# A scan feeding a cosine-gated layer: the opening re-ordered so that two of four sequences are scanned first

## The chip, the cores and the metric

The kernel runs on one core of a Trainium2 chip. The metric is the device time of one execution in microseconds (us); less is better. The kernel before the change took 381.69 us, the median of 7 runs (380.91 to 382.24).

## What is computed

The reference has two blocks. The first is a chunked state-space scan over `batch, heads, seq, head_dim, d_state = 4, 8, 768, 32, 16`:

```
cum = cumsum(log a);  L[i,j] = exp(cum_i - cum_j) for i >= j, else 0
y   = ((C B^T) * L) x  +  exp(cum) * (C state)
state = exp(sum log a) * state + sum_j exp(cum_end - cum_j) B_j x_j
```

Its output is laid out as 3072 tokens of 256 features. The second block is `h = x @ w_in` (256 x 2048), `g = h * cos(h)`, `out = g @ w_out` (2048 x 256). All tensors are fp32; the weights arrive as 64-bit words of which each fp32 value is put together on the chip.

## The kernel before the change

**Tiles.** The sequence is cut into 6 chunks of 128 steps. Each chunk gives 512 tokens (4 sequences of 128), and each chunk has 16 steps `n` of the second block. In chunk 0 one step `n` takes one pair of 128-wide `w_in` columns and one pair of sequences: even `n` takes sequences 0 and 1, odd `n` sequences 2 and 3 (`turn_of`). A step has three parts. `first(n)` is 4 matmuls into the PSUM bank `hp` (8 MATMUL records), then ACT rounds (`k`, L523) and DVE subtracts (`w`, L525). `gate(n)` is the sine on ACT (L530), and `gated(n)` the product on DVE (`gT`, L535). `second(n)` is the matmul by `w_out` (L578 in chunk 0), and it runs two steps behind (`LAG = 2`).

**The opening.** Before step 0, chunk 0 has to be scanned. For each sequence `b`: `spread_a` multiplies out the decays into PSUM; `decays0` runs the scan on DVE (L309) and then a copy and a memset on POOL (L312, L313); `cross` makes with one matmul, for two sequences, the part across halves, which ACT copies into `lam` (L321) and POOL weighs (`weigh`, L328); `turn` transposes B and C (L360) and ACT copies them out (L364, L366); `intra` makes `g = C B^T` on PE (L374) and `m = g * lam` on DVE (L381); `finish` makes `y` on PE (L391), which ACT copies to `yT` (L395).

**The weights.** `w_in` and `w_out` come in 8 pieces each, in 512 KB of words. `fetch` starts the transfer. `grade` is ACT's `Abs` (`mag`, L193), POOL's clamp (L194) and ACT's other half (`last`, L191). `join` is two bit operations on DVE (L207, L209) and an add on POOL (L217), after which the piece can be used. With `later=True` the `last` of a piece is issued behind the sine of the step. Piece `in 0` is needed by steps 0 and 1, `in 1` by steps 2 and 3, `out 0` by `second(0)` and `second(1)`.

**What sets the order.** The kernel is written under a manual schedule: every engine runs its instructions in the order in which they are written, and so does the one DMA queue on SP. An instruction that waits holds all behind it on its engine. PSUM banks go round in pairs under the tags `h`, `o` and `scan`. The order of the first step is written by hand at the end of the program (L669 ff.): all four `spread_a` and all four scans come first, then sequences 0, 1, 2, 3 through `turn`, `intra`, `finish`. POOL's two clamps of the decay rows (`cut`, `la`, L693 to L695) and the two transfers that write them to DRAM (`a_cut`, `a_all`, L697) stand between `finish(1)` and `join("in", 0)`. All later loads stand behind these two on SP: the rows of chunk 1 (B, C, x), `along` and `arow`, which read `a_all` and `a_cut` back, and the later pieces of the weights.

Of the kernel before, what the change touches and what calls it, by code (L numbers as in the profile page):

```python
# [8 lines left out]
FP32 = mybir.dt.float32  # L9
# [16 lines left out]
def kernel(  # L26
# [30 lines left out]
    V, ACT, G, PE = nc.vector, nc.scalar, nc.gpsimd, nc.tensor  # L57

    NB, H, S, D = x.shape
    N = B.shape[-1]  # L60
    P = 128
# [24 lines left out]
    def bank(shape, name, tag):  # L86
        return psum.tile(shape, FP32, tag=tag, bufs=2, name=name)

    def pair(name):

        return psum.tile([P, 2, 4 * P], FP32, tag="scan", bufs=2, name=name)
# [125 lines left out]
            G.tensor_tensor(out=dst.bitcast(U32), in0=bits, in1=last, op=ALU.add)  # L217

    for b in range(NB):
        if b == NB - 1:  # L220
            fetch("in", 0)
        load(0, (b, b + 1))
    nc.sync.dma_start(
# [70 lines left out]
    def spread_a(b, tag):  # L294


        spread[b] = ps = bank([P, H, W], "a_ps", tag)
        for t in range(2):
            PE.matmul(ps[t * W:(t + 1) * W], lhsT=those[:, b:b + 1].to_broadcast([P, W]),  # L299
                      rhs=a0s[:, t], start=True, stop=True, tile_position=(0, t * W),  # L300
                      skip_group_check=True)

    def decays0(b):

        lam[0, b] = l = scan.tile([P, 2, H, W], FP32, tag="lam", bufs=4, name="lam")
        flat = "p h i -> p (h i)"
        V.tensor_tensor_scan(out=l[:, 0].rearrange(flat), data0=spread.pop(b).rearrange(flat),  # L309
                             data1=unit0.rearrange(flat), initial=0.0,  # L310
                             op0=ALU.mult, op1=ALU.add)
        G.tensor_copy(out=l[W:P, 1], in_=l[W:P, 0])  # L312
        G.memset(l[W:P, 0], 0.0)  # L313

    def cross(b, tag):

        ps = bank([P, H, W], "l_ps", tag)
        PE.matmul(ps, lhsT=fros[:, b:b + 2].rearrange("p b j -> p (b j)"), rhs=tos,  # L318
                  start=True, stop=True)
        for t in range(2):  # L320
            ACT.copy(out=lam[0, b + t][0:W, 1], in_=ps[t * W:(t + 1) * W])  # L321
            weigh(0, b + t)

    def weigh(c, b):

        scaled[c, b] = sc = scan.tile([P, H, N], FP32, tag="sc", bufs=NB, name="sc")
        l = lam[c, b][:, :, P - 1:P] if c > 0 else lam[c, b][:, 1, :, W - 1:W]
        G.tensor_tensor(out=sc, in0=raw[c][0][:, 0, heads(b)],  # L328
                        in1=l.to_broadcast([P, H, N]), op=ALU.mult)
# [21 lines left out]
            return  # L351
        weigh(c, b)

    def turn(b, tag=None):

        bc = raw[0][0]
        tp = (pair("tp")[:, 0] if tag is None else bank([P, 4 * P], "tp", tag)
              ).rearrange("p (k i) -> p k i", k=4)
        for k in range(2):
            PE.transpose(tp[:, k], bc[:, k, heads(b)].rearrange("p h n -> p (h n)"), ident)  # L360

        cT = scan.tile([P, 2, P], FP32, tag="cT", name="cT")
        for t in range(2):
            ACT.activation(cT[:, t], tp[:, 1], AF.Copy, scale=slot[:, t:t + 1])  # L364
        bT = scan.tile([P, P], FP32, tag="bT", name="bT")
        ACT.copy(out=bT, in_=tp[:, 0])  # L366
        part[0, b] = (bT, cT)

    def intra(b):
        bT, cT = part[0, b]  # L370
        g = [pair("g") for _ in range(2)]
        for q in range(4):
            r = slice(32 * q, 32 * q + 32)
            PE.matmul(g[q // 2][:, q % 2, 0:2 * P], lhsT=bT[r],  # L374
                      rhs=cT[r].rearrange("p t (s i) -> p s t i", s=2), start=True, stop=True)
        l = lam.pop((0, b))
        m = scan.tile([P, 2, H, W], FP32, tag="m", bufs=4, name="m")
        for q in range(2):
            of = [t[:, :, q * HH:(q + 1) * HH].rearrange("p s (k t) i -> p k s (t i)", k=2)
                  for t in (m, l)]  # L380
            V.tensor_tensor(out=of[0], in0=g[q][:, :, 0:2 * P].rearrange(  # L381
                "p k (s i) -> p k s i", s=2), in1=of[1], op=ALU.mult)
        part[0, b] = m

    def finish(b, tag, fills=0):
        m, xr = part.pop((0, b)), raw[0][1]
        y = bank([P, 4, P], "y", tag)
        fill(y[:, 2:4], fills)
        for h in range(H):
            q, t = h % 4, h // 4  # L390
            PE.matmul(y[32 * q:32 * q + 32, t], lhsT=xr[:, b, h], rhs=m[:, :, h],  # L391
                      start=(t == 0), stop=True, tile_position=(0, 32 * q), skip_group_check=True)
        if b == 0:
            yT[0] = two.tile([P, 2, TB], FP32, tag="yT", name="yT")
        ACT.copy(out=yT[0][:, :, b * P:(b + 1) * P], in_=y[:, 0:2])  # L395
# [110 lines left out]
        c, f = divmod(n, NF)  # L506
        return (f % 2, f // 2) if c == 0 else divmod(f, NJ)

    def first(n):
        c, f = divmod(n, NF)  # L510
        hp[n] = bank([P, TB], "hp", "h")

        u, j = turn_of(n)
        to_ = hp[n].rearrange("p (e t s i) -> p e t s i", e=2, t=2, s=2)
        y = yT[c].rearrange("p k (u s t i) -> p k u t s i", u=2, s=2, t=2)
        for e in range(2):
            fs = slice((2 * j + e) * P, (2 * j + e + 1) * P)
            for k in range(KT):
                PE.matmul(to_[:, e], lhsT=w_in[:, k, fs], rhs=y[:, k, u],  # L519
                          start=(k == 0), stop=(k == KT - 1), skip_group_check=True)  # L520

        k = ffn.tile([P, TB], I32, tag="k", name="k")
        ACT.activation(k, hp[n], AF.Copy, bias=0.25, scale=INV_2PI)  # L523
        turns[n] = w = ffn.tile([P, TB], FP32, tag="w", name="w")
        V.scalar_tensor_tensor(out=w, in0=hp[n], scalar=INV_2PI, in1=k,  # L525
                               op0=ALU.mult, op1=ALU.subtract)

    def gate(n):
        cos = turns[n]
        ACT.activation(cos, cos, AF.Sin, bias=quarter, scale=TWO_PI)  # L530
# [139 lines left out]
    warm = bank([P, 4, P], "warm", "o")  # L670
    fill(warm, 2)
    spread_a(0, "h")
    turn(0)
    spread_a(1, "h")
    spread_a(2, "o")
    spread_a(3, "h")
    for b in range(NB):
        decays0(b)
    turn(1, "h")
    cross(0, "o")  # L680
    intra(0)
    turn(2, "h")
    cross(2, "o")
    intra(1)
    finish(0, "o")
    grade("in", 0, n=2)
    intra(2)
    turn(3, "h")
    finish(1, "o", 1)

    la = const.tile([RB, NU, P], FP32, name="la")
    cut = const.tile([RB, NU, P], FP32, name="cut")
# [4 lines left out]
        nc.sync.dma_start(  # L697
            out=dst.rearrange("(u b) h (c p) -> (b h c) u p", u=NU, p=P), in_=src)

    join("in", 0)  # L700
    finish(2, "o")
    intra(3)
    grade("in", 1)
    rest = grade("out", 0, later=True)
    join("in", 1)


    piece = {n: ("in", (n + 3) // 2) if n % 2 else ("out", n // 2) for n in range(NF)}
# [16 lines left out]

    def first_scan():

        finish(3, "o")
        for u in range(2):
            sums[u] = pair("s_ps")[:, :, 0:2 * D]  # L730
            for t in range(2):
                sum_up(0, 2 * u + t, sums[u][:, t])
# [25 lines left out]
    def ends(n):  # L758
        return [(c, us) for c, at, us, _, _, end in plan if at + end == n]

    rest_of_loads()
    for n in range(NC * NF + LAG):
        c, f = divmod(n, NF)
        if n < NC * NF:
            if f == 0 and c > 0:
                load(c + 2)
            first(n)
            if n == 0:
                first_scan()
            for at in pairs(n):  # L770
                turn2(*at)
            rests = [rest] if n == 0 else []
            if n + 1 in piece:
                rests.append(grade(*piece[n + 1], later=True))
            gate(n)
            for rest in rests:
                if rest:
                    rest()
            if n in piece and n > 1:
                join(*piece[n])  # L780

            behind = [lambda at=at: halved(*at) for at in halves_at(n)]
            behind = [lambda at=(c, 2 * u + 1): masked(*at) for c, u in pairs(n - 2)] + behind
            if n not in piece and behind:
                behind.pop(0)()
            gated(n)
            if n < 2:
                join(*piece[n])
            for do in (*behind, *unsummed):
                do()  # L790
            unsummed.clear()
            if n in (1, 2):
                carry(0, n - 1, sums[n - 1])
        for i, js in differ_at.get(n, ()):
            differ_w(i, js)
        if n >= LAG:
            second(n - LAG)
        for c, u in pairs(n - 1):
            intra2(c, u)
            masked(c, 2 * u)  # L800
        for c, us in ends(n):
            finish2(c, us)
            if 1 in us:
                raw.pop(c)
        for c, u in pairs(n + 1):
            for b in (2 * u, 2 * u + 1):
                reaches(c, b)
                load_along(c + 1, (b,))
# [30 lines left out]
```

## Time and profile before

| what | value |
|---|---|
| median of 7 runs | 381.69 us (380.91 to 382.24) |
| the profiled execution's own time | 380.91 us |
| its span | 379.1 us |
| around the span | 1.8 us |
| granted TensorE clock | 1.00 in every stretch |
| PE / DVE / ACT / POOL busy | 373.3 / 279.9 / 173.5 / 213.7 us |
| busy from 25.57 to 376.00 us (350.43 us): PE / DVE / ACT / POOL | 349.87 / 259.09 / 155.77 / 195.81 us |
| first `hp` matmul (step 0) | 17.68 us |
| first `o` matmul, `second(0)` | 25.57 us |

How to read it: times count from the span's start. A row of a timeline is start, duration, engine, line, operation, `output<-inputs`, shapes and count; the bracket at its end is the time for which the engine was idle before it and what ended that. In the chain of waits a row is start, duration and what the chain was in at that time. Matmul records are pipelined, so the first of a row looks longer than the work that it adds: 8 `hp` records behind others take 1.73 us. An fp32 matmul leaves two records.

### The profile page before, as it was taken

What the parts mean: (1) busy time and instruction counts of PE and PEld (TensorE: products, weight loads), DVE (VectorE), ACT (ScalarE), POOL (GpSimd) and SP (SyncE); (2) the same over time, 40 slices, a digit from 0 to 9 for tenths busy, and PEclk for the clock granted to TensorE, in tenths of its full rate; (3) what the DMA queues carried; (4) which work ended last, traced back from release to release, by engine and by line L of the source; (5) the groups of instructions that cost most, each with busy time, mean ns of one, the idle gap of its engine ahead of it and who ended that gap; (6) DMA issues with size and microseconds to landing.
All of it is one profiled execution on the core that took longest, in us unless ns stands there. A gap on an engine that the chain in (4) does not pass through costs nothing.

```text
span 379.1 us, 7680 instructions
## 1 busy us (share of the span) xinstructions
PE 373.3 (98%) x2980; PEld 330.2 (87%) x2980; DVE 279.9 (74%) x431; ACT 173.5 (46%) x303; POOL 213.7 (56%) x330
## 2 busy tenths in 40 slices
PE   8999999999999999999999999999999999999996
PEld 2578888889989999998999998899998999999995
DVE  8879999899689748967748986756986862554643
ACT  3887756444344434443434453424444433433442
POOL 6767565579864437673444683443775343454551
PEclk9999999999999999999999999999999999999999
DMA  6989989969230961420681330100010000010011
GB/s 79 259 235 292 251 209 129 180 96 176 78 110 17 148 61 58 138 73 2 83 74 55 83 117 11 42 2 2 1 30 3 8 21 2 0 29 0 2 28 29
DMA packets 106371, 30.42 MB, mean 80 GB/s; under 512 B 75520, under 2 KB 102240, under 8 KB 106336
## 3 DMA queue, kind: packets, MB, share of 16 engines
q1 hardware_dynamic: 106176, 29.81, 38.9%
q8 instruction: 23, 0.38, 0.5%
q10 hardware_dynamic: 160, 0.13, 0.1%
q14 instruction: 12, 0.10, 0.1%
HBM read 26.59 MB, written 3.34 MB: 79 GB/s over the span
## 4 chain that ended last, share of the span: by engine, by line
PE 96%; DVE 2%; POOL 1%; issue 0%; POOLq 0%
PE hp L519 43%; PE o L616 33%; PE o L578 7%; PE g L423 3%; PE y L457 3%; PE y L450 1%; PE tp L406 1%; PE a_ps L299 1%; PE warm L101 1%; DVE mag L209 1%; PE g L374 1%; POOL w_in L217 1%; PE o L661 1%; PE s_ps L478 0%; PE l_ps L318 0%; DVE mag L207 0%
## 5 line engine op out<-in xcount | busy, mean ns | idle before, releaser
L519 PE MATMUL hp<-yT,w_in 128*128 128x256 f32 x768 | 183.8, 382 | 0.5 <-POOL w_in L217 0.3
L519 PEld LDWEIGHTS hp<-yT,w_in 128*128 128x128 f32 x768 | 139.5, 190 | 21.4 <-issue 3.2
L560 POOL TENSOR_TENSOR gd<-gT 128x256 f32<-128x256 f32 x79 | 59.8, 757 | 104.9 <-DVE gT L535 79.5
L530 ACT ACTIVATE w<-w,quarter 128x512 f32<-128x512 f32 x96 | 69.3, 722 | 77.6 <-DVE w L525 77.4
L523 ACT ACTIVATE k<-hp 128x512 int32<-128x512 f32 x96 | 57.2, 596 | 103.3 <-PE hp L519 102.8
L525 DVE SCALAR_TENSOR_TENSOR w<-hp,k 128x512 f32<-128x512 f32 x96 | 65.7, 684 | 50.3 <-ACT k L523 50.1
L535 DVE TENSOR_TENSOR gT<-hp,w 128x512 f32<-128x512 f32 x96 | 65.2, 679 | 32.4 <-ACT w L530 27.2
L616 PE MATMUL o<-words,gd 128*128 128x128 f32 x474 | 66.9, 277 | 0.0
L616 PEld LDWEIGHTS o<-words,gd 128*128 128x128 f32 x474 | 59.8, 192 | 0.5
L345 DVE TENSOR_TENSOR_SCAN lam<-arow,unit 128x512 f32<-128x512 f32 x40 | 55.7, 1393 | 0.0
L563 POOL TENSOR_TENSOR gd<-gT,gd 128x128 f32<-128x128 f32 x79 | 48.1, 609 | 6.2
L616 PEld LDWEIGHTS o<-w_out,gT 128*128 128x128 f32 x316 | 46.9, 191 | 3.6
L616 PE MATMUL o<-w_out,gT 128*128 128x128 f32 x316 | 48.0, 275 | 0.0
L562 POOL TENSOR_TENSOR gd<-gT,gd 128x128 f32<-128x128 f32 x79 | 41.4, 525 | 6.2
L578 PE MATMUL o<-w_out,gT 128*128 128x256 f32 x128 | 30.3, 380 | 0.4 <-POOL w_out L217 0.4
L616 PE MATMUL o<-words,gT 128*128 128x128 f32 x158 | 30.6, 275 | 0.0
L616 PE MATMUL o<-w_out,gd 128*128 128x128 f32 x158 | 30.6, 275 | 0.0
L578 PEld LDWEIGHTS o<-w_out,gT 128*128 128x128 f32 x128 | 24.2, 190 | 4.0 <-POOL w_out L217 0.8
L436 DVE TENSOR_TENSOR m<-g,lam 128x512 f32<-128x512 f32 x40 | 25.6, 680 | 0.0
L616 PEld LDWEIGHTS o<-words,gT 128*128 128x128 f32 x158 | 24.0, 192 | 0.0
L616 PEld LDWEIGHTS o<-w_out,gd 128*128 128x128 f32 x158 | 24.0, 192 | 0.0
L633 DVE TENSOR_TENSOR sum<-ps,sum 128x256 f32<-128x256 f32 (+1 forms) x27 | 16.7, 645 | 0.6
(91 smaller groups left out, 281.7 us busy)
## 6 DMA issues: line engine op xcount, KB each, us to landing
arow<-a_cut SPq DMA_DIRECT2D x20, 512.0 KB, 4.0
words<-in_moe_w_in_dram SPq DMA_DIRECT2D x8, 512.0 KB, 6.3
words<-in_moe_w_out_dram SPq DMA_DIRECT2D x8, 512.0 KB, 8.5
out_dram<-sum SPq DMA_DIRECT2D x18, 128.0 KB, 2.5
xr<-in_x_dram SPq DMA_DIRECT2D x4, 512.0 KB
along<-a_all SPq DMA_DIRECT2D x20, 64.0 KB
xr<-in_x_dram SPq DMA_DIRECT2D x8, 128.0 KB
bc<-in_B_dram SPq DMA_DIRECT2D x4, 256.0 KB, 5.1
```

The costliest lines, as they stand in the source:

```text
L345: V.tensor_tensor_scan(out=lam[c, b][:, hs].rearrange("p h i -> p (h i)"), data0=rows_.rearrange("p h i -> p (h i)"), data1=unit.rearrange ...
L436: V.tensor_tensor(out=of[0], in0=g[q][:, :, s * 2 * P:(s + 1) * 2 * P], in1=of[1], op=ALU.mult)
L519: PE.matmul(to_[:, e], lhsT=w_in[:, k, fs], rhs=y[:, k, u], start=(k == 0), stop=(k == KT - 1), skip_group_check=True)
L523: ACT.activation(k, hp[n], AF.Copy, bias=0.25, scale=INV_2PI)
L525: V.scalar_tensor_tensor(out=w, in0=hp[n], scalar=INV_2PI, in1=k, op0=ALU.mult, op1=ALU.subtract)
L530: ACT.activation(cos, cos, AF.Sin, bias=quarter, scale=TWO_PI)
L535: V.tensor_tensor(out=gT[n], in0=hp.pop(n), in1=cos, op=ALU.mult)
L560: G.tensor_tensor(out=d[:, 0:2], in0=g[:, 1:2].to_broadcast([P, 2, P]), in1=g[:, 3::-3], op=ALU.subtract)
L562: G.tensor_tensor(out=d[:, 2], in0=g[:, 0], in1=d[:, 0], op=ALU.subtract)
L563: G.tensor_tensor(out=d[:, 3], in0=g[:, 2], in1=d[:, 2], op=ALU.subtract)
L578: PE.matmul(o[c, u][:, t], lhsT=g[:, 2 * e + t], rhs=w_out[:, 2 * j + e], start=(j == e == t == 0), stop=(j == NJ - 1 and e == 1), skip_gr ...
L616: PE.matmul(at[q], lhsT=a_[q], rhs=w[q], start=(j == 0 and q in starts), stop=(j == NJ - 1), skip_group_check=True)
```

## The change

Sequences 0 and 1 are carried through scan, `turn`, `intra` and `finish` first. The scan of sequence 2 follows `intra(0)`, that of sequence 3 follows `join("in", 0)`; `spread_a(2)` and `spread_a(3)` move back with them. `turn(2)` and `turn(3)` are issued together behind that, then `intra(2)`. `cross` no longer contains ACT's copies and POOL's `weigh`; the copies are `crossed(b)`, and `weigh` is issued later. On SP, `in 0` is fetched before sequence 2 and no longer before sequence 3. `grade("in", 0)` moves up, `join("in", 0)` moves up to before the scan of sequence 3.

On POOL the clamp of `in 1` now stands before `cut` and `la`; `weigh(0, 0)` and `weigh(0, 1)` follow these, then the clamp of `out 0`, the add of `in 1`, `weigh(0, 2)` and `weigh(0, 3)`, the clamp of `in 2` and the add of `out 0`. Step 0 gets a function of its own, `start`: `intra(3)` lies between the two tiles of `first(0)`; `join("in", 1)`, ACT's and DVE's part of step 0 (`turned`), `finish(2)` and `finish(3)` follow; and `join("out", 0)` stands before `gated(0)` where it stood behind it. `first_scan` (the matmuls `s_ps` of the state) moves from behind `first(0)` to behind `first(1)`. The filling matmul of `finish(1)` goes. `turn` takes its bank from the caller, with half the width.

```diff
--- before.py
+++ after.py
@@ -217,7 +217,7 @@
             G.tensor_tensor(out=dst.bitcast(U32), in0=bits, in1=last, op=ALU.add)
     for b in range(NB):
-        if b == NB - 1:
+        if b == 2:
             fetch("in", 0)
         load(0, (b, b + 1))
     nc.sync.dma_start(
@@ -300,11 +300,16 @@
                       rhs=a0s[:, t], start=True, stop=True, tile_position=(0, t * W),
                       skip_group_check=True)
-    def decays0(b):
-        lam[0, b] = l = scan.tile([P, 2, H, W], FP32, tag="lam", bufs=4, name="lam")
+    def decays0(b, early=False):
+        if early:
+            lam[0, b] = scan.tile([P, 2, H, W], FP32, tag="lam", bufs=4, name="lam")
+            return
+        if (0, b) not in lam:
+            decays0(b, True)
+        l = lam[0, b]
         flat = "p h i -> p (h i)"
         V.tensor_tensor_scan(out=l[:, 0].rearrange(flat), data0=spread.pop(b).rearrange(flat),
                              data1=unit0.rearrange(flat), initial=0.0,
@@ -312,14 +317,17 @@
         G.tensor_copy(out=l[W:P, 1], in_=l[W:P, 0])
         G.memset(l[W:P, 0], 0.0)
+    crosses = {}
     def cross(b, tag):
         ps = bank([P, H, W], "l_ps", tag)
         PE.matmul(ps, lhsT=fros[:, b:b + 2].rearrange("p b j -> p (b j)"), rhs=tos,
                   start=True, stop=True)
-        for t in range(2):
-            ACT.copy(out=lam[0, b + t][0:W, 1], in_=ps[t * W:(t + 1) * W])
-            weigh(0, b + t)
+        crosses.update({b + t: ps[t * W:(t + 1) * W] for t in range(2)})
+    def crossed(b):
+        ACT.copy(out=lam[0, b][0:W, 1], in_=crosses.pop(b))
     def weigh(c, b):
@@ -351,11 +359,10 @@
             return
         weigh(c, b)
-    def turn(b, tag=None):
+    def turn(b, tp):
         bc = raw[0][0]
-        tp = (pair("tp")[:, 0] if tag is None else bank([P, 4 * P], "tp", tag)
-              ).rearrange("p (k i) -> p k i", k=4)
+        tp = tp.rearrange("p (k i) -> p k i", k=2)
         for k in range(2):
             PE.transpose(tp[:, k], bc[:, k, heads(b)].rearrange("p h n -> p (h n)"), ident)
@@ -373,7 +380,7 @@
             r = slice(32 * q, 32 * q + 32)
             PE.matmul(g[q // 2][:, q % 2, 0:2 * P], lhsT=bT[r],
                       rhs=cT[r].rearrange("p t (s i) -> p s t i", s=2), start=True, stop=True)
-        l = lam.pop((0, b))
+        l = lam[0, b]
         m = scan.tile([P, 2, H, W], FP32, tag="m", bufs=4, name="m")
         for q in range(2):
             of = [t[:, :, q * HH:(q + 1) * HH].rearrange("p s (k t) i -> p k s (t i)", k=2)
@@ -506,7 +513,7 @@
         c, f = divmod(n, NF)
         return (f % 2, f // 2) if c == 0 else divmod(f, NJ)
-    def first(n):
+    def first(n, between=None):
         c, f = divmod(n, NF)
         hp[n] = bank([P, TB], "hp", "h")
@@ -514,10 +521,16 @@
         to_ = hp[n].rearrange("p (e t s i) -> p e t s i", e=2, t=2, s=2)
         y = yT[c].rearrange("p k (u s t i) -> p k u t s i", u=2, s=2, t=2)
         for e in range(2):
+            if e and between:
+                between()
             fs = slice((2 * j + e) * P, (2 * j + e + 1) * P)
             for k in range(KT):
                 PE.matmul(to_[:, e], lhsT=w_in[:, k, fs], rhs=y[:, k, u],
                           start=(k == 0), stop=(k == KT - 1), skip_group_check=True)
+        if not between:
+            turned(n)
+    def turned(n):
         k = ffn.tile([P, TB], I32, tag="k", name="k")
         ACT.activation(k, hp[n], AF.Copy, bias=0.25, scale=INV_2PI)
@@ -670,23 +683,32 @@
     warm = bank([P, 4, P], "warm", "o")
     fill(warm, 2)
     spread_a(0, "h")
-    turn(0)
+    turn(0, pair("tp")[:, 0, 0:2 * P])
     spread_a(1, "h")
+    decays0(0)
+    decays0(1)
+    cross(0, "o")
+    crossed(0)
+    crossed(1)
+    intra(0)
+    turn(1, bank([P, 2 * P], "tp", "h"))
+    grade("in", 0, n=2)
     spread_a(2, "o")
+    decays0(2)
+    intra(1)
+    cross(2, "o")
     spread_a(3, "h")
-    for b in range(NB):
-        decays0(b)
-    turn(1, "h")
-    cross(0, "o")
-    intra(0)
-    turn(2, "h")
-    cross(2, "o")
-    intra(1)
+    decays0(3, early=True)
+    crossed(2)
+    crossed(3)
     finish(0, "o")
-    grade("in", 0, n=2)
+    finish(1, "o")
+    join("in", 0)
+    decays0(3)
+    turn(2, bank([P, 2 * P], "tp", "h"))
+    turn(3, bank([P, 2 * P], "tp", "o"))
     intra(2)
-    turn(3, "h")
-    finish(1, "o", 1)
+    grade("in", 1)
     la = const.tile([RB, NU, P], FP32, name="la")
     cut = const.tile([RB, NU, P], FP32, name="cut")
@@ -697,12 +719,8 @@
         nc.sync.dma_start(
             out=dst.rearrange("(u b) h (c p) -> (b h c) u p", u=NU, p=P), in_=src)
-    join("in", 0)
-    finish(2, "o")
-    intra(3)
-    grade("in", 1)
-    rest = grade("out", 0, later=True)
-    join("in", 1)
+    weigh(0, 0)
+    weigh(0, 1)
     piece = {n: ("in", (n + 3) // 2) if n % 2 else ("out", n // 2) for n in range(NF)}
@@ -725,7 +743,6 @@
     def first_scan():
-        finish(3, "o")
         for u in range(2):
             sums[u] = pair("s_ps")[:, :, 0:2 * D]
             for t in range(2):
@@ -758,20 +775,41 @@
     def ends(n):
         return [(c, us) for c, at, us, _, _, end in plan if at + end == n]
+    def start():
+        rests = [grade("out", 0, later=True)]
+        first(0, lambda: intra(3))
+        join("in", 1)
+        turned(0)
+        finish(2, "o")
+        for b in range(NB):
+            if b > 1:
+                weigh(0, b)
+            del lam[0, b]
+        finish(3, "o")
+        rests.append(grade(*piece[1], later=True))
+        gate(0)
+        for rest in rests:
+            if rest:
+                rest()
+        join("out", 0)
+        gated(0)
     rest_of_loads()
+    start()
     for n in range(NC * NF + LAG):
         c, f = divmod(n, NF)
         if n < NC * NF:
             if f == 0 and c > 0:
                 load(c + 2)
+            if n == 0:
+                continue
             first(n)
-            if n == 0:
+            if n == 1:
                 first_scan()
             for at in pairs(n):
                 turn2(*at)
-            rests = [rest] if n == 0 else []
-            if n + 1 in piece:
-                rests.append(grade(*piece[n + 1], later=True))
+            rests = [grade(*piece[n + 1], later=True)] if n + 1 in piece else []
             gate(n)
             for rest in rests:
                 if rest:
@@ -784,7 +822,7 @@
             if n not in piece and behind:
                 behind.pop(0)()
             gated(n)
-            if n < 2:
+            if n == 1:
                 join(*piece[n])
             for do in (*behind, *unsummed):
                 do()
```

## The prediction

> **What bounds the kernel now.** I read the page's chain first, then the busy time of the long stretch, then the chain of waits in the first 40 us, then POOL, ACT and SP there in order of time.
>
> ```profile
> span 379.1 us, 7680 instructions
> ...
> PE 96%; DVE 2%; POOL 1%; issue 0%; POOLq 0%
> ```
>
> The end hangs on PE almost throughout. The busy time of each engine from the first `o` matmul on (stretch, length, then PE, PEld, DVE, ACT, POOL):
>
> ```profile
> 25.57:376.00 350.43, 349.87 (x2794) 318.25 (x2794) 259.09 (x394) 155.77 (x262) 195.81 (x294) 1.00 0.36 71
> ```
>
> PE is busy for 349.87 of 350.43 us, and nothing there is changed. So the change can gain or lose only by the moment at which `second(0)` starts, 25.57 us, and by a hole that it tears behind that. The chain ahead of it:
>
> ```profile
> 18.87 0.63 POOL mag L194
> ...
> 21.05 1.27 POOL w_in L217
> 22.32 0.59 POOL mag L194
> ...
> 24.25 1.28 POOL w_out L217
> 25.53 0.04 issue
> 25.57 1.99 PE o L578 x8
> 27.57 1.73 PE hp L519 x8
> ```
>
> Not the scan but the weights end last: clamp of `in 1`, its add, clamp of `in 2`, add of `out 0`. What they wait for in turn stands on ACT and in the transfers (issue to landing, last column):
>
> ```profile
> 17.21 0.66 ACT L193 ACTIVATE mag<-words 128x512 f32<-128x512 f32 x1
> ...
> 18.75 0.70 ACT L193 ACTIVATE mag<-words 128x512 f32<-128x512 f32 x1 [0.30 <-DMA words<-in_moe_w_out_dram]
> ```
>
> ```profile
> words<-in_moe_w_in_dram SPq DMA_DIRECT2D x1, 512.0 KB, 4.3
> ```
>
> `in 1` is issued at 12.89 and lands 4.3 later, at 17.19; ACT takes it at 17.21. `out 0` is awaited at 18.75. Both are set by the loads, not by the scan. The DMA engines are busy at a share near 1 from 10 to 25 us.
>
> **What goes away, priced at its place.** `first(0)` needs `yT` of two sequences and `w_in` piece 0, whose second half is added at 18.06 to 18.79. Now `in 0` is fetched ahead of sequence 2's B, C and x, its join no longer stands behind `intra(2)` and `turn(3)`, and two scans (1.2 each, four in 4.80) leave the path to `m(0)`. Working the opening through with the rows of before (scan 1.2, POOL copy and memset 0.61 + 0.52, ACT's copies of a turn 0.78, `m` 1.29, half-piece joins 0.28 + 0.43 and 0.73 on POOL), I get both halves of piece 0 by about 15.1, the first tile of `first(0)` at about 15.7 instead of 17.68, POOL's last memset done by about 16.7, the last of `finish` at about 19.3. All that is some 2 us ahead of the rows of before, and is cover rather than gain: the next thing POOL has to do waits for `in 1` at 17.19. The fill of `finish(1)` (0.60) lay in the opening too, and is worth nothing where PE waits; the narrower banks of `turn` and ACT's copies on their own change no instruction's length.
>
> **What POOL has to do from there.** Before:
>
> ```profile
> 18.87 1.55 POOL L194 TENSOR_SCALAR mag<-mag 128x512 f32<-128x512 f32 x2
> 21.05 1.27 POOL L217 TENSOR_TENSOR w_in<-mag,last 128x512 uint32<-128x512 uint32 x1 [0.63 <-DVE mag L209]
> 22.29 0.61 POOL L194 TENSOR_SCALAR mag<-mag 128x512 f32<-128x512 f32 x1
> 24.25 1.27 POOL L217 TENSOR_TENSOR w_out<-mag,last 128x512 uint32<-128x512 uint32 x1 [1.35 <-DVE mag L209]
> ```
>
> It had 0.63 and 1.35 of idle time in this stretch, waiting for DVE; `cut`, `la` and the four `weigh` had been done by 16.83. After the change all of these stand in the queue behind the clamp of `in 1`. In order, with about 0.06 between two of POOL's instructions: ACT's `mag` ends at 17.87 and POOL starts 0.09 later, as it did for `in 0` (14.35 to 14.44). Clamp `in 1` 0.61, to 18.57. `cut` 0.40, memset 0.13, `la` 0.60, to 19.90. `weigh` of 0 and 1, spaced 0.37 with 0.41 for the last (three took 1.15), to 20.73. Clamp `out 0` 0.61, to 21.40. Add `in 1` 1.27, to 22.72. `weigh` of 2 and 3, to 23.55. Clamp `in 2` 0.61, to 24.21. Add `out 0` 1.27, to 25.53, and PE 0.04 later: **25.57, the very moment of before**. Before, POOL lost 0.91 (17.96 to 18.87), 0.63 and 1.35 here, 2.89 in all; the moved work is 1.33 + 0.83 + 0.83 = 2.99 and fills just that. DVE is not late for any of it: join `in 1` about 18.7 to 20.1 (0.43 + 0.98), join `out 0` about 21.5 to 22.9, ahead of its add at 24.26.
>
> **PE beside it.** `s_ps` now follows `first(1)` and needs `weigh(0, 3)`, done at 23.55. `first(2)` and `second(0)` are queued behind it on PE. A quarter of 0.63 is left, 0.16, and `first(2)` is 1.73 in a dense stream and 1.97 in its own row of before (23.19): `second(0)` at 25.5 to 25.8. `first(2)` also needs `gT(0)`, which now stands behind join `out 0`: sine about 22.2, join done about 22.9, product to 23.5. That is level and costs nothing.
>
> **Collisions of POOL and DVE.** The bit operation L209 on 128x512 takes 0.69 while POOL is idle (23.41) and 0.98 while POOL clamps (19.98), and the two clamps beside it took 1.55 instead of 1.25. POOL's queue is now dense, so both joins fall into it. Lower bound 0 (DVE does all the waiting), upper bound twice 0.3 from that pair. I take 0.25, as before mostly DVE was the one that waited. The Trainium skill speaks here against the change: "SBUF — State Buffer", section "SBUF: two separate sides", has DVE and GpSimd share a port pair that one instruction holds to its end, when a DVE instruction has two SBUF inputs or runs in a two-port mode. By that rule POOL could wait out both joins whole, twice some 1.1, and the sum would be two microseconds later; the pair at 18.87 lost 0.3, so the row decides.
>
> **Sum.** 25.57 + 0.25 = about 25.8, with PE's own 25.5 to 25.8 beneath it: +0.3. Span 379.1 to 379.4, the profiled execution 380.91 to 381.2. It lies 0.8 below the median of the runs, so against the median: 381.69 + 0.3 = **382.0**.
>
> **SP's queue.** `a_cut` and `a_all` wait for `cut` and `la`, now done at 19.03 and 19.90.
>
> ```profile
> 16.17 0.33 SPq L697 DMA_DIRECT2D a_cut<-cut  x1
> 16.85 0.45 SPq L697 DMA_DIRECT2D a_all<-la  x1
> 17.35 0.46 SPq L168 DMA_DIRECT2D words<-in_moe_w_out_dram  x1
> 17.87 0.51 SPq L119 DMA_DIRECT2D bc<-in_B_dram  x1
> 18.74 4.00 SPq L119 DMA_DIRECT2D bc<-in_C_dram  x1
> 22.79 3.14 SPq L119 DMA_DIRECT2D xr<-in_x_dram  x1
> ```
>
> They come 3 us later, and so do `out 2` and all loads of chunk 1 behind them. I cost that at nothing, because the C load held the queue for 4.00 where another such issue took 0.58: it waits for room, that is for data moved earlier, and would be reached at about 21.5, still ahead of 22.74. If that cover is false, the rival below gives the price.
>
> **Rivals.**
> *Later by the queue of SP (0.15).* If the 4.00 is the issue's own, `in 4` (issued at 27.31, landing at 32.9 by its landing record) lands up to 2.8 later. ACT takes it at 33.34 ahead of the sine of step 4, and the product of step 4 ends at 36.12 for `hp` of step 6 at 37.93. The product moves to about 37.9, a scan of 1.91 follows on DVE, and the product of step 5 (40.18, for `hp` of step 7 at 41.38) comes at about 42. One hole of about 0.6, perhaps a second like it: +0.9 to +1.5 in all, 382.6 to 383.2. It decides as soon as `in 4` lands over 1.5 later. Slower.
> *Later by collisions (0.15).* The clamp L194 takes 0.61 alone and up to 0.93 in the first 60 us. If all three clamps of the queue are held so, that is 3 x 0.32 on top of the 0.25, or 0.6 to 1.0 with `cut` and `la` in part: +0.8 to +1.3, 382.5 to 383.0. It decides from an end of add `out 0` past 26.3. Slower.
> *Earlier by the loads (0.20).* The x load of sequence 3 held SP for 2.21 where the first three took 0.58; `in 0` lay just ahead of it. With `in 0` moved up, `in 1` could be issued 1.63 sooner. By the landing records it came 2.28 behind `a_in` (14.91), while `out 0` came 1.53 behind `in 1`; at that pace it lands 0.75 sooner, or 1.15 if the x load too moves up by 0.4. POOL, done with the scan at 16.7, could follow: 380.5 to 380.95. Against it: bytes and packets ahead of `in 1` are the same, and the DMA share is near 1. Even with earlier weights PE needs about 24.9 (`k(0)` behind the awaited `out 0`, `yT` 20.75, then 1.8, 0.63, 1.73), unless `out 0` lands earlier too.
> *No gain, no loss (0.50)* is the forecast: 381.4 to 382.4. The change does what it says, step 0 starts 2 us earlier, and `second(0)` does not.
>
> **How the numbers follow.** The measurement tells about 0.2% from no change, here 0.76: 380.93 to 382.45. The forecast's 0.50 and 0.02 of the rival by the loads lie within; 0.18 of that rival is faster; both later rivals are slower, 0.30. The range reaches into the early rival to 380.6 and to the end of the late ones at 383.2.
>
> **What would show it.** Right: first `hp` near 15.7; POOL without idle time from 18 to 25.5; the first `o` at 25.6 to 26.0 released by POOL's add or behind `s_ps`; PE dense behind it. Wrong: POOL idle in that stretch, a landing of `in 1` well off 17.2, or PE idle near 35 to 45 with ACT waiting for `words`.

## The result, and the profile after

The changed kernel takes 382.39 us, the median of 15 runs (381.38 to 384.81), against 381.64 us of the kernel before beside it. The ratio is 1.0028, 95% interval 1.0018 to 1.0037. The time lies in the predicted range, but the forecast was too small: +0.3 us was expected, within what can be told from no change. What came is +0.75 us by the medians and about +1 us (0.28%) by the ratio. The ratio compares means, and the one run at 384.81 makes 0.05% of it; without it the means give 1.0023. The page of the changed kernel:

```profile
span 380.9 us, 7681 instructions
...
PE 92%; SPq 3%; POOL 2%; DMA 1%; issue 0%; ACT 0%; DVE 0%; POOLq 0%
```

Before, the chain was PE for 96%. Now SP (which issues the transfers one after the other), a transfer and POOL hold the first part of it. The stretch behind the opening (columns as before) is as dense as it was:

```profile
26.00:376.00 350.00, 350.00 (x2798) 318.69 (x2797) 257.95 (x392) 156.72 (x263) 196.87 (x295) 1.00 0.37 71
```

So all of the difference lies ahead of `second(0)`. The chain there:

```profile
12.91 4.87 DMA words<-in_moe_w_in_dram
17.78 0.02 issue
17.81 0.68 ACT mag L193
...
18.63 0.61 POOL mag L194
...
19.32 0.41 POOL cut L715
...
20.12 0.86 POOL la L717
...
21.07 0.79 POOL sc L336 x2
...
21.94 0.61 POOL mag L194
22.55 1.24 POOL w_in L217
23.79 1.38 POOL sc L336 x2
25.21 0.36 PE s_ps L485 x8
25.58 0.06 issue
25.64 1.97 PE hp L528 x8
27.61 1.73 PE o L591 x8
```

These rows begin with the transfer of `in 1`; ahead of it the chain is SP's issuing of the loads. From the clamp of `in 1` on it is POOL without a gap: clamp, `cut`, `la`, two weighs (`sc`), clamp, add, two weighs. Then PE: the last quarter of `s_ps`, `first(2)`, `second(0)`. Two rows of PE show the wait for the weighs, three of DVE what became of the join of `out 0` and of `gT(0)` behind it:

```profile
24.40 0.32 PE L485 MATMUL s_ps<-xr,sc 128*32 128x64 f32 x8 [1.04 <-POOL sc L336]
25.21 0.32 PE L485 MATMUL s_ps<-xr,sc 128*32 128x64 f32 x8 [0.50 <-POOL sc L336]
```

```profile
22.58 1.49 DVE L207 TENSOR_SCALAR mag<-mag 128x512 uint32<-128x512 uint32 x1 [1.25 <-POOL mag L194]
24.11 0.78 DVE L209 SCALAR_TENSOR_TENSOR mag<-words,mag 128x512 uint32<-128x512 uint32 x1
24.82 0.68 DVE L548 TENSOR_TENSOR gT<-hp,w 128x512 f32<-128x512 f32 x1
```

L207 takes 0.42 in its next row (27.49), beside an idle POOL, and 1.49 here, where POOL's add of `in 1` runs from 22.52 to 23.79 and a weigh follows.

**Two traces are not two medians.** In the chain `o` starts at 27.61 against 25.57, but the first is drawn behind another row (1.73 long) and the second behind idle time (1.99). By the ends of the two rows `second(0)` is 1.77 later, and the profiled executions, 382.66 and 380.91, differ by 1.75. In 13 of the 14 kept traces the time is the end of this `o` row plus 353.34 us, within 0.03, so this moment alone sets it. The medians differ by only 0.75, the ratio by about 1.07. Both traces are of executions with a short opening (first `a_ps` row 1.08 in both). The first `a_ps` rows of two executions, of the kernel before, and of the same kernel with only one load moved (below):

```profile
4.72 1.08 PE L299 MATMUL a_ps<-a0s,those 128*64 128x512 f32 x4
```

```profile
4.77 1.98 PE L299 MATMUL a_ps<-a0s,those 128*64 128x512 f32 x4
```

The same four records take 1.08 in one execution and 1.98 in another, and what follows on PE starts 0.95 later. In the second of these executions `second(0)` starts at 26.68 and the time is 381.99. The runs of the kernel before spread over 380.55 to 382.24, which fits. Those of the changed kernel do not spread so: 13 of 15 lie between 382.25 and 382.72.

### The profile page after: what moved, and what is told of

The parts are those of the page before. It is cut to its first block, busy times and chain, and to the rows that moved or that the text cites. A ratio compares the mean times of both kernels' runs of the same rounds, so it can differ in the third digit from the quotient of the medians.

```text
span 380.9 us, 7681 instructions
## 1 busy us (share of the span) xinstructions
PE 373.2 (98%) x2978; PEld 329.8 (87%) x2978; DVE 280.9 (74%) x431; ACT 173.4 (46%) x303; POOL 214.5 (56%) x330
## 4 chain that ended last, share of the span: by engine, by line
PE 92%; SPq 3%; POOL 2%; DMA 1%; issue 0%; ACT 0%; DVE 0%; POOLq 0%
PE hp L528 44%; PE o L629 33%; PE o L591 7%; PE g L430 3%; PE y L464 3%; SPq L119 2%; PE y L457 1%; DMA words<-in_moe_w_in_dram 1%; PE tp L413 1%; POOL sc L336 1%; PE s_ps L485 1%; PE o L674 1%; POOL w_in L217 0%; POOL mag L194 0%; SPq L168 0%
## 5 line engine op out<-in xcount | busy, mean ns | idle before, releaser
L591 PEld LDWEIGHTS o<-w_out,gT 128*128 128x128 f32 x128 | 24.3, 190 | 3.2
```

The lines of the kernel that those rows point to most:

```text
L591: PE.matmul(o[c, u][:, t], lhsT=g[:, 2 * e + t], rhs=w_out[:, 2 * j + e], start=(j == e == t == 0), stop=(j == NJ - 1 and e == 1), skip_gr ...
```

## The experiments

Theory A: POOL's queue from the clamp of `in 1` on, with the moved `cut`, `la` and weighs in it and the wait of `s_ps` for the last weigh, sets `second(0)`. Rivals: the later landing of `in 1` (B); collisions of POOL with DVE's joins (C); later `gT(0)` behind the join of `out 0` (D). Each time stands beside runs of the kernel before on the same chip, so that ratios are compared. The changed kernel has 1.0028, and differences to it are taken from that; from 1.0023 (without the run at 384.81) they would be 0.2 us smaller.

**cut and la ahead of the clamp of `in 1`.**

```diff
     intra(2)
-    grade("in", 1)
     la = const.tile([RB, NU, P], FP32, name="la")
...
             out=dst.rearrange("(u b) h (c p) -> (b h c) u p", u=NU, p=P), in_=src)
+    grade("in", 1)
     weigh(0, 0)
```

> The changed kernel with one thing undone: POOL's cut and la, and the two transfers behind them, stand ahead of the clamp of in 1 again. In the changed kernel POOL was idle for 1.39 us ahead of that clamp and spent 1.74 us on cut and la behind it (19.24 to 20.98). Theory A (POOL's queue from the clamp of in 1 sets second(0)): the queue is 1.6 to 1.74 shorter, second(0) about 26.0 instead of 27.6, time 1.2 to 1.7 us below the changed kernel, about 0.997 of it. Theory B (the later landing of in 1 alone, 17.78 against 17.19): POOL's queue has room, no difference, at most 0.2. Theory C (collisions of POOL with DVE's joins): cut and la leave the join of in 1, the memset and la take 0.13 and 0.40 to 0.60 again instead of 0.26 and 0.86, but the weighs move into the joins, so 0.4 us at most.

Measured: 381.83 us, ratio 1.0014 (1.0004 to 1.0023), about 0.5 below the changed kernel. A's direction, less than half of its size. In its trace the opening was a long one (`a_ps` 1.98), POOL reached the clamp only at 19.39, and the weighs still held `s_ps` until 24.66: `o` at 27.05.

**The weighs where their inputs are ready.**

```diff
     crossed(1)
+    weigh(0, 0)
+    weigh(0, 1)
...
     crossed(3)
+    weigh(0, 2)
...
-    weigh(0, 0)
-    weigh(0, 1)
+    weigh(0, 3)
...
-            if b > 1:
-                weigh(0, b)
```

> The changed kernel with one thing undone: the weighs are issued where their inputs are ready (0 and 1 behind the copies of sequences 0 and 1, 2 behind those of 2 and 3, 3 ahead of the clamp of out 0). Theory A: POOL's queue loses three weighs, 0.39 each without collision, and 0.6 of collision, and s_ps no longer waits for a weigh at 25.2: second(0) about 25.4 to 26.2 instead of 27.6, time 1.4 to 2.2 us below the changed kernel. Theory B (landing of in 1): no difference. Theory C (collisions alone): 0.6 below.

Measured: 381.98 us, ratio 1.0017 (1.0008 to 1.0025), about 0.4 below. `s_ps` waited no more, but `first(2)` did not start behind it. The chain of this kernel names what came instead:

```profile
21.38 0.61 POOL mag L194
22.01 1.50 DVE mag L207
...
23.54 0.98 DVE mag L209
...
24.52 0.61 DVE gT L548
...
25.27 1.97 PE hp L528 x8
```

The join of `out 0`, 2.48 instead of 1.1, stands ahead of `gT(0)`, whose bank `first(2)` needs. This is theory D, formed here. The time by itself does not exclude C, which expected 0.6.

**`in 1` fetched ahead of sequence 3.**

```diff
-        if b == 2:
-            fetch("in", 0)
+        if b > 1:
+            fetch("in", b - 2)
...
-    for w in (("in", 1), ("out", 0), ("in", 2), ("out", 1), ("in", 3)):
+    for w in (("out", 0), ("in", 2), ("out", 1), ("in", 3)):
```

> The changed kernel with in 1 fetched ahead of sequence 3's B, C and x, right behind sequence 2's. in 1 should land near 14.5 and sequence 3's x near 16.2. Theory A with its start at the landing of in 1: POOL's clamp of in 1 moves from 18.63 to about 17.3, where POOL becomes free, and second(0) with it: 1.0 to 1.4 us below the changed kernel. Theory B (the landing alone is the loss): the 0.6 by which it came later, so 0.6 below. If neither: the later rows of sequence 3 hold turn(3) and first(0), and the time is the same or up to 0.5 above.

Measured: 382.55 us (5 runs, 382.35 to 382.57), ratio 1.0031 (1.0019 to 1.0043): no gain. `in 1` was issued at 9.75 instead of 12.91, ACT took it at 16.98 without waiting for it, and the time stayed. (Of its time some 0.15 to 0.2 us lie outside the span, 1.95 us there against 1.8 in the other kernels, for a reason that no run shows; the spans too are no shorter than those of the changed kernel, 380.6 us in the median of both.) In its trace the opening was long (`a_ps` 1.97), the chain ran through it and the scan, and from 21.16 on through the clamp of `out 0`, the add of `in 1` and the weighs to `o` at 27.15. So the landing of `in 1` alone does not set the time: it and the opening end close together, and the queue behind both stays as long as it was. Theory B falls as the whole cause; what a short opening would give here, no trace shows.

**The kernel before, with only the order of the loads changed.**

```diff
-        if b == NB - 1:
+        if b == 2:
             fetch("in", 0)
```

> The kernel before with one thing of the change alone: in 0 is fetched ahead of sequence 2's loads. Theory A: nothing, as POOL there reaches the clamp of in 1 only at 18.87, behind the adds of in 0; within 0.3 us of the kernel before. Theory B (the order of the loads lets in 1 land 0.6 later, and this costs): up to 0.6 above.

Measured: 381.55 us, ratio 1.0004 (0.9994 to 1.0013): nothing, as A says. `in 1` landed at about 17.5 in its trace.

**Both undone.** The edits of the first two together.

> The changed kernel with both undone: cut and la ahead of the clamp of in 1, and the weighs where their inputs are ready. Theory A (POOL's queue behind the clamp of in 1, with the weighs that s_ps waits for): the two gains add up nearly, second(0) about 26.3 where POOL's queue begins late (19.4) and 25.6 where it begins at the landing of in 1: 0.9 to 1.5 us below the changed kernel, level with the kernel before or 0.5 below it. Theory D (gT(0) behind the join of out 0 on DVE, which loses 1.0 to POOL's add of in 1, is the next limit): no more than the 0.5 that each gave alone.

Measured: 381.85 us, ratio 1.0016 (1.0007 to 1.0025): no better than either alone, as D says. In its trace L207 took 1.12 beside the add of `in 1`, and `first(2)` waited for `gT` until 24.89.

**Both undone, and the join of `out 0` behind the product.**

```diff
-        join("out", 0)
         gated(0)
+        join("out", 0)
```

> As the kernel with both undone, and the join of out 0 behind the product of step 0 as in the kernel before. Theory D: gT(0) is done near 23 and first(2) starts behind s_ps near 23.6, second(0) then waits for the add of out 0 alone, about 25.7: 0.3 to 0.7 us below the kernel with both undone, 0.5 to 1.0 below the kernel before. Theory A alone: the same as with both undone, as the add of out 0 comes no earlier.

Measured: 381.05 us, ratio 0.9997 (0.9986 to 1.0007). The whole loss is gone. D's gain against both undone is 0.19%, 0.7 us, the upper end of what was expected; the hoped-for gain over the kernel before did not come. Its DVE, POOL and PE:

```profile
22.46 0.69 DVE L548 TENSOR_TENSOR gT<-hp,w 128x512 f32<-128x512 f32 x1 [0.79 <-ACT w L543]
23.07 0.42 DVE L207 TENSOR_SCALAR mag<-mag 128x512 uint32<-128x512 uint32 x1
```

```profile
24.36 1.27 POOL L217 TENSOR_TENSOR w_out<-mag,last 128x512 uint32<-128x512 uint32 x1 [1.35 <-DVE mag L209]
```

```profile
23.15 0.65 PE L485 MATMUL s_ps<-xr,sc 128*32 128x64 f32 x32
23.73 1.99 PE L528 MATMUL hp<-yT,w_in 128*128 128x256 f32 x8
25.68 1.99 PE L591 MATMUL o<-w_out,gT 128*128 128x256 f32 x8
```

L207 is back at 0.42, `s_ps` and `first(2)` follow without a wait, and the add of `out 0` ends at 25.63, with PE at 25.68. PE and POOL now end together, so the earlier scan has nothing left to buy.

**Only the join of `out 0` behind the product.** The last edit alone, on the changed kernel.

> The changed kernel with one thing undone: the join of out 0 stands behind the product of step 0 again. Theory A: POOL's queue and the wait of s_ps for the last weigh (25.2) stay, at most 0.3 us below the changed kernel, by fewer collisions. Theory D alone: gT(0) comes 2 us sooner and first(2) with it, 0.5 to 1.5 below.

Measured: 382.1 us, ratio 1.002 (1.001 to 1.0029), 0.3 below: A's bound as a number, but not by A's path. In its trace:

```profile
24.01 0.65 PE L485 MATMUL s_ps<-xr,sc 128*32 128x64 f32 x32
25.67 1.26 POOL L217 TENSOR_TENSOR w_out<-mag,last 128x512 uint32<-128x512 uint32 x1 [0.69 <-DVE mag L209]
```

The last two weighs took 0.78 and not 1.41 and were done at 24.22: `s_ps` waited for none. `first(2)` started at 24.59, and `second(0)` waited for the add of `out 0` until 26.99, as the join now came later and POOL waited for it.

**The two remaining pairs.** Weighs and product:

> The changed kernel with two things undone: the weighs where their inputs are ready, and the join of out 0 behind the product of step 0. cut and la stay behind the clamp of in 1. The weighs alone gave 0.42 us, with gT(0) behind the join as the next limit. Theory A with D: first(2) starts behind s_ps near 23.5, and the add of out 0 comes behind cut and la near 26: 0.6 to 1.2 us below the changed kernel, 1.000 of the kernel before. If cut and la alone hold POOL, no more than the 0.42.

Measured: 381.79 us, ratio 1.0006 (0.9996 to 1.0016), some 0.8 below the changed kernel, as expected. `cut`, `la` and product:

> The changed kernel with two things undone: cut and la ahead of the clamp of in 1, and the join of out 0 behind the product of step 0. The weighs stay late, so s_ps waits for the last of them near 24.3 and first(2) and second(0) behind it. Theory A with D: 0.5 to 0.9 us below the changed kernel, not as much as with the weighs undone too (1.2).

Measured: 381.57 us, ratio 1.0004 (0.9994 to 1.0014), some 0.9 below: the upper end of what was expected. The other pair was expected to give a little more and did not; the intervals overlap. The expected wait of `s_ps` near 24.3 did not come either: it ran from 22.89 without one, and `second(0)` waited for the add of `out 0` until 25.92.

**The kernel before, with only `cut` and `la` late.**

```diff
-    la = const.tile([RB, NU, P], FP32, name="la")
...
     join("in", 0)
     finish(2, "o")
     intra(3)
     grade("in", 1)
+    la = const.tile([RB, NU, P], FP32, name="la")
...
```

> The kernel before with one thing of the change alone: cut, la and their two transfers behind the clamp of in 1. Theory A: POOL there has 2 us of idle time between the clamp of in 1 and the add of out 0 (0.63 and 1.35), and the 1.33 goes into it: 0 to 0.4 us above the kernel before. Rival (the later transfers on SP starve the loads of chunk 1 and the weights): 0.6 to 1.5 above.

Measured: 381.39 us, ratio 1.0007 (0.9997 to 1.0018): within A's 0 to 0.4. In its trace `o` came at 26.05, 0.5 later than in that of before, with an opening 0.4 longer (`a_ps` 1.46). The same move that costs about 0.5 in the changed kernel costs about 0.3 here, where POOL had 2 us of idle time; the intervals are too wide to tell the two apart. The rival of the later transfers asked for 0.6 or more.

**Without the filling matmuls at the start.** In both kernels.

```diff
-    fill(warm, 2)
+    fill(warm, 0)
```

> The changed kernel without the two filling matmuls at the start, so that TensorE starts its real work cold in every run. In the traces so far the first a_ps group takes 1.08 us in some runs and 1.98 in others, and all that follows is later by the difference. Theory E (the changed kernel hangs on the landing of in 1 and POOL, with 1.4 us of POOL idle time ahead of it, so that it neither gains from a warm opening nor loses much by a cold one): the opening is 1.7 to 3.4 us longer than the warm one, of which 1.4 is hidden: 0.3 to 2.0 us above the changed kernel. Rival (the opening sets the time of both kernels alike): the same loss as for the kernel before.

Measured, the changed kernel: 382.94 us, ratio 1.0045 (1.0029 to 1.006), so 0.17% or 0.65 us over the changed kernel, whose interval overlaps with this one. In its trace step 0 starts at 17.30 instead of 16.19, and yet POOL reaches the clamp of `in 1` no later than the changed kernel (18.63):

```profile
18.45 0.61 POOL L194 TENSOR_SCALAR mag<-mag 128x512 f32<-128x512 f32 x1
```

> The kernel before without the two filling matmuls at the start. Theory E: its chain begins in the opening, so all of the longer opening shows against its warm runs (380.7), and 1.3 to 2.9 us against its median; it ends level with the changed kernel without them, or above it. Rival: the distance of the two kernels stays at 0.28%.

Measured, the kernel before: 383.33 us, ratio 1.0048 (1.0032 to 1.0064), so 0.48% or 1.8 us. In its trace all of the longer opening arrives at `second(0)`, which starts 1.69 later than in the trace of before:

```profile
27.26 1.99 PE o L578 x8
```

By these numbers a cold start costs the kernel before about three times as much, and the two kernels end level. The rival, a distance that stays at 0.28%, would put the changed kernel at 1.0076, beyond its interval. This is theory E: the change did make the opening cheap, by the cover that was predicted, and this shows only where the opening is long. The opening itself was expected to be 1.7 to 3.4 longer; by the first `hp` row it was 1.1 (changed kernel) and 1.6 (19.26 against 17.68).

All eight combinations of the three undone parts, as ratios to the kernel before:

| cut, la early | weighs early | product first | ratio |
|---|---|---|---|
| no | no | no | 1.0028 |
| yes | no | no | 1.0014 |
| no | yes | no | 1.0017 |
| no | no | yes | 1.0020 |
| yes | yes | no | 1.0016 |
| yes | no | yes | 1.0004 |
| no | yes | yes | 1.0006 |
| yes | yes | yes | 0.9997 |

## Why the prediction was right and where it was not

**Right.** PE behind `second(0)` is dense, and the change counts only by that moment (350.00 of 350.00). Step 0's first tile came early: 16.19 against 17.68, half a microsecond later than worked out. POOL was idle for 1.39 ahead of the clamp of `in 1`, as the cover said, and then ran from 18.63 to 26.98 without idle time, in the order of the sum. SP's queue was costed at nothing, and that holds. Its rows now:

```profile
20.07 0.33 SPq L719 DMA_DIRECT2D a_cut<-cut  x1
...
22.89 0.58 SPq L119 DMA_DIRECT2D bc<-in_C_dram  x1
23.52 1.69 SPq L119 DMA_DIRECT2D xr<-in_x_dram  x1
```

`a_cut` came 3.9 later, yet the C load took 0.58 where it had held the queue for 4.00, and `along` was issued at 25.31 instead of 26.03. The 4.00 was waiting, and the delay went into it, though the cover was thinner than worked out: the C load was reached at 22.89, not 21.5. The rival by SP's queue is refuted.

**Wrong in size.** The prediction summed POOL up to the last weigh at 23.55; it was 25.17. The 1.62 are, term by term: the landing of `in 1` 0.59 (17.78; in other traces with that order of loads between 16.9 and 18.1); `cut`, memset and `la` 1.74 instead of 1.33, 0.41; the last two weighs 1.38 instead of 0.83, 0.55; the rest 0.07. So collisions cost POOL about 1.0, and 0.25 was taken. They were bounded from one pair of clamps that had lost 0.3. But the join of `in 1` (DVE 19.38 to 20.73) met three of POOL's instructions and that of `out 0` the add and two weighs, one after the other. Behind that weigh the path on PE was mis-sized too: the last quarter of `s_ps` was taken at 0.16, and from the weigh's end to `first(2)` it was 0.47 (25.17 to 25.64). 23.55 + 1.62 + 0.47 + 1.97 is the 27.61 at which `o` starts; POOL's own add of `out 0`, which the forecast had as the last thing to wait for, ended 0.6 earlier, at 26.98.

**Wrong in a step.** "`gT(0)`, which now stands behind join `out 0` [...] level and costs nothing" failed. The join was taken at 1.1 to 1.4 and took 2.3, `gT(0)` ended at 25.50 instead of 23.5, just ahead of `first(2)`. Alone it is hidden behind the weighs; undone last, it is worth 0.7 us. The rule of the Trainium skill that was weighed there ("SBUF — State Buffer", "SBUF: two separate sides") was set aside by the row of the clamps. DVE's L207 at 1.49 and 1.50 beside POOL's add of 1.27, against 0.42, agrees with it in kind: L207 ends 0.28 behind the end of the add. That L207, with one tensor input, is a case of the rule (its two-port modes) no run shows. By the rule the loss would have been over two microseconds on POOL; POOL lost 1.0 and DVE's join 1.2, so here both lost, and the row of the clamps was too low a bound.

**Not seen, and luck.** The forecast took the profiled execution as typical, 0.8 below the median though it was, and added a difference to the median. No trace of a slower run of before was kept, but with the moved load, which changes nothing in the time, `second(0)` starts at 26.68 and not at 25.57; if the slower runs of before are like that one, the same later moment costs less against the median than between the two traces. Two errors, collisions taken too small and an execution with a short opening as the base, worked against each other. That 382.39 came out so near to 382.0 is luck as far as the size goes: for the profiled execution 381.2 was forecast and 382.66 measured. By the prediction's own sign, an end of the add of `out 0` past 26.3 (it was 26.98), its rival of later collisions came, which it gave 0.15 and priced at 382.5 to 383.0.

The cause is settled as far as the three parts go: undone together they give back the whole loss, singly 0.08 to 0.14% each. With intervals of about 0.1% to either side none of the three is clear of noise by itself, so the share of each stays open. Nor do the runs separate A from C: every move that shortens POOL's queue also takes POOL's work out of DVE's joins, and of the 1.62 above about 1.0 is collisions.

## What to carry to other kernels

Before work is pulled ahead, follow the engine that the next late transfer feeds, and count what else has been moved into its queue: idle time that is bought ahead of a transfer is of use only if the moved work is put into it and not behind. Two engines that are both dense can lose to each other far more than one pair of collisions in a sparse stretch shows: here about 1.0 on POOL against the 0.3 of the pair. And before a difference of a few tenths of a per cent is worked out from one trace, look at how the runs spread and whether that trace is a typical one.

## What the runs showed of the hardware that was not expected

The first four `a_ps` records took between 1.08 and 1.98 us (1.30, 1.46, 1.50 and 1.72 among them) in traces of kernels whose work up to there is the same. The granted clock of 1.00 "in every stretch" does not speak against a slow clock there: the clock record that each trace holds begins only where full speed is granted, and the views give 1.00 ahead of it too. Full speed begins at 4.61 us in the trace of before, at 4.78 in that of the changed kernel and at 6.82 in that of the moved load, where `a_ps` takes 1.08, 1.08 and 1.98. Over the twelve traces with filling matmuls it begins between 4.33 and 7.10, and from 4.78 to 6.76 `a_ps`, which starts near 4.77, grows with it from 1.08 to 1.98. At that moment single records get shorter: the 128x512 ones of `a_ps` take 1.06 to 1.12 us ahead of it (moved load) and 0.59 to 0.64 behind it. Without the filling it begins at 7.59 and 8.41. The stretch at full speed lasts 375.47 or 372.05 us in all 14 traces, and these are 110 and 109 times their difference of 3.41. The Trainium skill, "TensorE: Matmul & The Clock Gate", section "Part 1: The HAM clock gate", has a cold TensorE at half its clock until a window of some 3.4 us of activity is over, with windows that run freely, so that the moment differs from run to run. The near doubling, the spread and the two lengths, one window apart, agree with that; what decides in which window full speed begins no run here shows. And a DVE bit operation with one tensor input (L207) waited beside POOL's add for about the length of that add, 1.49 against 0.42.
